# A split DMA transpose and chunked products for one batch, between two tiles of a fused attention and snake-MLP kernel

## The chip, the cores and the metric

The kernel runs on one core of one Trainium2 chip. The metric is the device time of one execution in microseconds, the median of several runs. The profile is of one execution and counts time from the start of its span, 294.8 us, which is a little shorter than the run's time.

Names used below: TensorE (PE in the profile, its weight loads PEld), VectorE (DVE), ScalarE (ACT), GpSimd (POOL), and SyncE (SP), which issues most of the DMAs. SBUF is the on-chip memory, PSUM the accumulator memory that TensorE writes.

## The reference

Linear attention over 8 batches of 8 heads, 576 tokens and 64 features a head, followed by an MLP on the 8 x 576 = 4608 tokens of 512 features:

```python
q_s = softmax(q, axis=-1)                 # over the 64 features
k_s = softmax(k, axis=2)                  # over the 576 tokens
kv  = einsum('bhsd,bhse->bhde', k_s, v)   # 64 x 64 for each head
a   = einsum('bhsd,bhde->bhse', q_s, kv)  # 576 x 64 for each head
x   = a.transpose(0, 2, 1, 3).reshape(4608, 512)
h   = x @ w_in                            # 512 -> 2048
g   = h + sin(alpha * h) ** 2 / alpha
out = g @ w_out                           # 2048 -> 512
```

(The reference also subtracts the maximum before each exponential and adds 1e-9 to the divisors.)

## The kernel before

The MLP works on nine tiles of 512 tokens. For each tile it makes 16 slots `h` of 128 x 512 (four matmuls each, the "first product", into PSUM tiles `hp`), a sine and a square, the combination `g`, and then four blocks of the output, 16 matmuls each (the "second product", PSUM tiles `op`). The attention of a batch has 576 tokens, 9 groups of 64; its result goes transposed into `xT`, from which the first product reads. Batch 2 fills columns 1152 to 1727 of `xT`, tile 2 reads columns 1024 to 1535.

The parts that the change touches:

```python
    def norm_q(b, engs):                       # softmax's division for q
        qe = A["qe", b]
        A["qn", b] = qn = att1.tile([128, J, 4 * D], BF16, name="qn")      # att1: one buffer
        qs = small.tile([128, J, 4], F32, name="qs")
        n = len(engs)
        w = 4 // n
        for h in range(n):
            cols = slice(h * w * D, (h + 1) * w * D)
            ...
            nc.vector.tensor_reduce(part, src, axis=AXL.X, op=ALU.add)
            nc.vector.reciprocal(part, part)
            engs[h].tensor_tensor(dst, src, part.unsqueeze(3).to_broadcast([128, J, w, D]), op=ALU.mult)

    TP = ((0, 6), (6, 9))

    def q_transpose(b, g, pool, eng):          # on TensorE, for batches 0 and 1
        ...
        for j in range(j0, j1):
            h, jj = divmod(j - j0, 3)
            for ii in range(2):
                nc.tensor.transpose(tp[:, h, 2 * jj + ii], qn[:, j, ii * 128:(ii + 1) * 128], identb)
        eng(qT[:, j0:j1].rearrange("p (h jj) ii c -> p h (jj ii) c", h=m), tp[:, 0:m, 0:6])

    def q_transpose_dma(b):                    # by DMA, for batches 2 to 7
        A["qT", b] = att2.tile([128, J, 2, 128], BF16, name="qT")
        nc.sync.dma_start(out=A["qT", b].rearrange("p j ii c -> p (j ii) c"),
                          in_=A["qn", b].rearrange("p j c -> p (j c)"), transpose=True)

    XO = ((0, 4), (4, 9))

    def attn_out(b, ii, half, pool, eng):      # q times kv: two matmuls and one evacuation
        qT, kt = A["qT", b], kbd[b % 2]
        j0, j1 = XO[half]
        n = (j1 - j0) * P                      # P = 64
        xp = pool.tile([128, 2, 512], F32, name="xp", tag="a")
        for e in range(2):
            nc.tensor.matmul(xp[:, e, 0:n], kt[:, e, ii], qT[:, j0:j1, ii, e * 64:(e + 1) * 64],
                             start=True, stop=True)
        c0 = (J * b + j0) * P
        eng(xT[:, 2 * ii:2 * ii + 2, c0:c0 + n], xp[:, :, 0:n])

    ...
    ps_h = ctx.enter_context(tc.tile_pool(name="ps_h", bufs=4, space=PSUM, reuse_waits="tile"))
    ps_o = ctx.enter_context(tc.tile_pool(name="ps_o", bufs=2, space=PSUM, reuse_waits="tile"))
    ps_a = ctx.enter_context(tc.tile_pool(name="ps_a", bufs=1, space=PSUM, reuse_waits="tile"))
    ...
    # between the first product of tile 1 and that of tile 2
    exp_q(2)
    exp_k(2)
    os = o_stream(1)                           # tile 1's 64 output matmuls, taken in parts
    take(os, 16)
    norm_q(2, [GP, V])
    exp_q(3)
    exp_k(3)
    load("v", v, 3)
    q_transpose_dma(2)
    cast_v(3, [GP, GP])
    nc.scalar.activation(zero, zero, AX.Sin)
    take(os, 16)
    kv_mm(2, 0, ps_a)
    kv_mm(2, 1, ps_a)
    kv_norm(2)
    norm_q(3, [GP])
    take(os, 26)
    for n in range(4):
        attn_out(2, n // 2, n % 2, ps_a, ACT_CP)
        take(os, (2, 2, 1, 1000)[n])
    q_transpose_dma(3)
    load_batch(4)
    ...
    for ni in range(nN):                       # tile 2's first product
        h_slot(2, ni, SQ2[ni], lag, lent)
        ...
```

Instructions of one engine run in the order of the program. The `evac_o` inside `o_stream` empties each output block with VectorE and issues two output DMAs.

Of the kernel before, what the change touches and what calls it, by code (L numbers as in the profile page):

```python
# [15 lines left out]
F32 = mybir.dt.float32  # L16
BF16 = mybir.dt.bfloat16
AX = mybir.ActivationFunctionType
ALU = mybir.AluOpType
AXL = mybir.AxisListType  # L20
# [3 lines left out]
def kernel(  # L24
# [14 lines left out]
    nc = tc.nc  # L39
    ctx.enter_context(nc.allow_non_contiguous_dma(reason="layout"))  # L40
    B, H, S, D = q.shape
# [3 lines left out]
    J = 9  # L45
    P = S // J
    nN = d_ff // 128
    MF = 512
# [7 lines left out]
    att1 = ctx.enter_context(tc.tile_pool(name="att1", bufs=1))  # L56
    att2 = ctx.enter_context(tc.tile_pool(name="att2", bufs=2))
# [8 lines left out]
    identb = singles.tile([128, 128], BF16, name="identb")  # L66
    xT = singles.tile([128, 4, NT], BF16, name="xT")
# [5 lines left out]
    kbd = [singles.tile([128, 2, 2, 128], BF16, name=f"kbd{n}") for n in range(2)]  # L73
    vb = [singles.tile([128, J, 4 * 65], BF16, name=f"vb{n}") for n in range(2)]

    def src_view(t, b):
        return t[b].rearrange("(i e) (p j) d -> (e p) i (j d)", e=2, j=J)
# [5 lines left out]
    staged = {}  # L83

    def load(name, t, b, halves=False, eng=nc.sync):
        st = stage.tile([128, 4, J, D], F32, name=f"st_{name}", tag="st")
        view = src_view(t, b)
        flat = st.rearrange("p i j d -> p i (j d)")
        if halves:
            for ii in range(2):  # L90
                eng.dma_start(out=flat[:, ii::2], in_=view[:, ii::2])
        else:
            eng.dma_start(out=flat, in_=view)
        staged[name, b] = st

    def load_batch(b):
        load("q", q, b)
        load("k", k, b)
        load("v", v, b)
# [6 lines left out]
    def load_wout(c):  # L106
        nc.gpsimd.dma_start(out=wout[:, 4 * c:4 * c + 4, :], in_=wout_v[:, 4 * c:4 * c + 4, :])


    A = {}  # L110
# [6 lines left out]
    def exp_q(b):  # L117
        A["qe", b] = att2.tile([128, J, 4 * D], BF16, name="qe")
        exp_to(A["qe", b], staged["q", b])
# [5 lines left out]
    def cast_v(b, engs):  # L125
        vv = vb[b % 2].rearrange("p j (i c) -> p i j c", i=4)
        for ii in range(2):
            engs[ii].tensor_copy(vv[:, 2 * ii:2 * ii + 2, :, 0:D], staged["v", b][:, ii::2])  # L128

    def norm_q(b, engs):  # L130

        qe = A["qe", b]
        A["qn", b] = qn = att1.tile([128, J, 4 * D], BF16, name="qn")
        qs = small.tile([128, J, 4], F32, name="qs")
        n = len(engs)
        w = 4 // n
        for h in range(n):
            cols = slice(h * w * D, (h + 1) * w * D)
            src = qe[:, :, cols].rearrange("p j (i d) -> p j i d", i=w)
            dst = qn[:, :, cols].rearrange("p j (i d) -> p j i d", i=w)  # L140
            part = qs[:, :, h * w:(h + 1) * w]
            nc.vector.tensor_reduce(part, src, axis=AXL.X, op=ALU.add)  # L142
            nc.vector.reciprocal(part, part)  # L143
            engs[h].tensor_tensor(dst, src, part.unsqueeze(3).to_broadcast([128, J, w, D]), op=ALU.mult)  # L144

    def kv_mm(b, ii, pool, split=False):

# [21 lines left out]

    TP = ((0, 6), (6, 9))  # L170

    def q_transpose(b, g, pool, eng):
        if g == 0:
            A["qT", b] = att2.tile([128, J, 2, 128], BF16, name="qT")
        qn, qT = A["qn", b], A["qT", b]
        j0, j1 = TP[g]
        m = (j1 - j0) // 3
        tp = pool.tile([128, 2, 8, 128], BF16, name="tp", tag="a")
        for j in range(j0, j1):
            h, jj = divmod(j - j0, 3)  # L180
            for ii in range(2):
                nc.tensor.transpose(tp[:, h, 2 * jj + ii], qn[:, j, ii * 128:(ii + 1) * 128], identb)
        eng(qT[:, j0:j1].rearrange("p (h jj) ii c -> p h (jj ii) c", h=m), tp[:, 0:m, 0:6])  # L183

    def q_transpose_dma(b):
        A["qT", b] = att2.tile([128, J, 2, 128], BF16, name="qT")
        nc.sync.dma_start(out=A["qT", b].rearrange("p j ii c -> p (j ii) c"),
                          in_=A["qn", b].rearrange("p j c -> p (j c)"), transpose=True)

    XO = ((0, 4), (4, 9))  # L190

    def attn_out(b, ii, half, pool, eng):
        qT, kt = A["qT", b], kbd[b % 2]
        j0, j1 = XO[half]
        n = (j1 - j0) * P
        xp = pool.tile([128, 2, 512], F32, name="xp", tag="a")
        for e in range(2):
            nc.tensor.matmul(xp[:, e, 0:n], kt[:, e, ii], qT[:, j0:j1, ii, e * 64:(e + 1) * 64],  # L198
                             start=True, stop=True)
        c0 = (J * b + j0) * P  # L200
        eng(xT[:, 2 * ii:2 * ii + 2, c0:c0 + n], xp[:, :, 0:n])  # L201


    G = {}
# [40 lines left out]
                                                         in_=o[64 * hf:64 * hf + 64, cols])  # L245


    ACT_CP, DVE_CP = nc.scalar.copy, nc.vector.tensor_copy
    V, GP = nc.vector, nc.gpsimd
    nc.scalar.dma_start(out=alpha_rows, in_=moe_alpha.rearrange("(no ni) -> no ni", ni=128))  # L250
    load("q", q, 0, halves=True)
# [3 lines left out]
    for ii, j0, j1 in VJ:  # L255
        nc.sync.dma_start(out=st[:, ii::2, j0:j1].rearrange("p i j d -> p i (j d)"),
                          in_=src_view(v, 0)[:, ii::2, j0 * D:j1 * D])
# [48 lines left out]
    ps_h = ctx.enter_context(tc.tile_pool(name="ps_h", bufs=4, space=PSUM, reuse_waits="tile"))  # L306

    def h_slot(t, ni, sq, lag, wide=None):
        hp = mm_h(t, ni, wide)
        lag.append((t, ni, hp, sine(t, ni, hp, sq)))  # L310

    def flush(lag, keep):
        while len(lag) > keep:
            combine(*lag.pop(0))
# [14 lines left out]
    def take(it, n=1000):  # L329
        for _ in range(n):  # L330
            if next(it, 0) == 0:
                return
# [4 lines left out]
    with tc.tile_pool(name="ps_e", bufs=2, space=PSUM, reuse_waits="tile") as ps_e:  # L337
        def lent():
            return ps_e.tile([128, 2, MF], F32, name="hh", tag="a")[:, 0]

        late = {3: ("q", q, 1, True), 6: ("k", k, 1, False), 8: ("v", v, 1, True)}
        for ni in range(nN):
            h_slot(0, ni, "PAPDPAPADPAPPDAP"[ni], lag, lent)
            flush(lag, 1)
            if ni in late:
                name, x, b, hv = late[ni]
                load(name, x, b, halves=hv, eng=GP)
            if ni == 11:
                load_wout(3)
        flush(lag, 0)  # L350

        exp_q(1)
        norm_q(1, [GP, V])
        exp_k(1)
        cast_v(1, [GP, GP])
        for name, x in (("q", q), ("k", k), ("v", v)):
            load(name, x, 2, eng=GP)
        accs = [ps_h.tile([128, dm], F32, name="hp", tag="h") for _ in range(4)]
        os = o_quad(0, accs, [DVE_CP, ACT_CP, DVE_CP, ACT_CP])
        take(os, 44)  # L360
        q_transpose(1, 0, ps_e, ACT_CP)
        nc.scalar.activation(zero, zero, AX.Sin)
        take(os, 2)
        q_transpose(1, 1, ps_e, DVE_CP)
        take(os, 2)
        kv_mm(1, 0, ps_e)
        kv_mm(1, 1, ps_e)
        kv_norm(1)
        take(os, 6)
        for ii in range(2):  # L370
            attn_out(1, ii, 0, ps_e, DVE_CP)
            attn_out(1, ii, 1, ps_e, ACT_CP)
            take(os, 3)
        take(os)
        load("q", q, 3)
        load("k", k, 3)

        for ni in range(nN):
            h_slot(1, ni, SQ[ni], lag, lent)
            flush(lag, 1)  # L380
        cast_v(2, [GP, GP])
        flush(lag, 0)

    ps_o = ctx.enter_context(tc.tile_pool(name="ps_o", bufs=2, space=PSUM, reuse_waits="tile"))
    ps_a = ctx.enter_context(tc.tile_pool(name="ps_a", bufs=1, space=PSUM, reuse_waits="tile"))
# [14 lines left out]
    os = o_stream(1)  # L400
# [2 lines left out]
    exp_q(3)  # L403
    exp_k(3)
    load("v", v, 3)
    q_transpose_dma(2)
    cast_v(3, [GP, GP])
    nc.scalar.activation(zero, zero, AX.Sin)
    take(os, 16)
    kv_mm(2, 0, ps_a)  # L410
    kv_mm(2, 1, ps_a)
    kv_norm(2)
    norm_q(3, [GP])
    take(os, 26)
    for n in range(4):
        attn_out(2, n // 2, n % 2, ps_a, ACT_CP)
        take(os, (2, 2, 1, 1000)[n])
    q_transpose_dma(3)
    load_batch(4)

# [18 lines left out]
    for t in range(3, nT):  # L439
        b = t + 1 if t + 1 < B else None  # L440
        os = o_stream(t - 1)
        done = 0
        for ni in range(nN):
            hp = mm_h(t, ni)
            if b is not None:
                if ni == 4:
                    q_transpose_dma(b)
                attn_back(b, ni - 5)
            s = sine(t, ni, hp, "A")
            combine(t, ni, hp, s)  # L450
            if b is not None and ni == 0:
                exp_q(b)
                exp_k(b)
                cast_v(b, [GP, GP])
                norm_q(b, [GP])
                if b + 1 < B:
                    load_batch(b + 1)
            want = 23 + 21 * ni // 8 if b is not None else 4 * (ni + 1)
            take(os, min(64, want) - done)
            done = min(64, want)  # L460
        take(os)

    take(o_stream(nT - 1), 48)
    for h in range(2):
        cols = slice(h * 256, h * 256 + 256)
# [34 lines left out]
```

The softmax here doesn't subtract the row's maximum and nothing guards it: scores larger than these inputs give would overflow.

## Time and profile before

| what | value |
|---|---|
| time, median of 3 runs | 296.62 us (296.46 to 296.97) |
| span of the profiled execution | 294.8 us |
| TensorE matmuls busy | 279.5 us, 95% |
| ScalarE busy | 228.1 us, 77% |
| VectorE busy | 185.9 us, 63% |
| GpSimd busy | 84.6 us, 29% |
| the six DMA transposes, issue to landing | 4.6 to 5.7 us, median 5.1 |
| the v load of batch 3 | issued at 69.30 us, used from 75.19 us |

In the lines quoted below, L187 is the DMA transpose (`qT<-qn`), L198 the products of q and kv (`xp`), L201 their evacuation into `xT`, L215 the first product (`hp`), L235 the second product (`op`), L142 to L144 the normalisation of q. An entry "x26" is a run of 26 instructions shown as one. Where square brackets end a line they give how long the engine stood idle before it and what it waited for. A busy TensorE is not TensorE at its peak, because matmuls are pipelined; the pitch from one to the next is shorter than the duration shown for one.

### The profile page before, as it was taken

The numbers are of one execution on the slowest core, as the hardware profiler recorded it, in microseconds if no ns is written. First come the engines' busy times: TensorE is split into PE (matmuls) and PEld (weight loads), VectorE is DVE, ScalarE is ACT, GpSimd is POOL, SyncE is SP. The second block draws the span as 40 slices with busy tenths as digits, with TensorE's granted clock in tenths as the row PEclk, the third lists the DMA queues.
The fourth block names the chain that finished last, engine by engine and source line by source line (L and its number), as shares of the span: only waits on it lengthen the run. The fifth ranks groups of instructions, "written<-read, shape, count | busy, mean of one in ns | idle before, by whom it ended". The sixth has DMA issues, their size and how long they took to land.

```text
span 294.8 us, 4250 instructions
## 1 busy us (share of the span) xinstructions
PE 279.5 (95%) x1576; PEld 132.4 (45%) x1576; DVE 185.9 (63%) x270; ACT 228.1 (77%) x320; POOL 84.6 (29%) x73
## 2 busy tenths in 40 slices
PE   2999999999799999999999999999999999999994
PEld 1544445444344444444444444444444444444443
DVE  3758955789638857865687568756875455555421
ACT  4679855999578899879987999799977777777500
POOL 0939590575665536000700061005000000000000
PEclk9999999999999999999999999999999999999999
DMA  7999989955859986108921794112411111111143
GB/s 261 281 191 207 366 234 364 390 189 165 183 85 323 392 282 139 28 21 290 330 50 36 235 337 98 36 39 60 91 38 36 36 36 38 36 36 37 46 99 72
DMA packets 35221, 45.77 MB, mean 155 GB/s; under 512 B 15856, under 2 KB 19712, under 8 KB 35200
## 3 DMA queue, kind: packets, MB, share of 16 engines
q1 hardware_dynamic: 29600, 34.09, 40.6%
q0 software_dynamic: 5408, 11.27, 14.9%
q8 instruction: 12, 0.20, 0.3%
q10 hardware_dynamic: 192, 0.14, 0.2%
q14 instruction: 9, 0.07, 0.1%
HBM read 36.71 MB, written 9.44 MB: 157 GB/s over the span
## 4 chain that ended last, share of the span: by engine, by line
PE 75%; DVE 9%; ACT 5%; POOL 3%; DMA 3%; issue 2%; ACTq 0%; SPq 0%
PE op L235 31%; PE hp L215 30%; PE hp L235 4%; DVE g L231 3%; PE xp L198 3%; PE warm L279 2%; POOL s L225 2%; DVE xT L201 2%; ACT s L221 2%; PE kvp L154 2%; DMA qT<-qn 2%; DMA st_q<-in_q_dram 1%; DVE o L241 1%; ACT xT L201 1%; PE op L468 1%
## 5 line engine op out<-in xcount | busy, mean ns | idle before, releaser
L231 DVE SCALAR_TENSOR_TENSOR g<-s,inva_sb,hp 128x512 bf16<-128x512 f32 x130 | 95.3, 746 | 65.1 <-ACT s L223 52.3
L215 PE MATMUL hp<-xT,win 128*128 128x512 bf16 x520 | 129.7, 379 | 0.3
L235 PE MATMUL op<-wout,g 128*128 128x512 bf16 x496 | 123.8, 379 | 0.0
L221 ACT ACTIVATE s<-hp,alpha_sb 128x512 f32<-128x512 f32 x130 | 87.8, 682 | 27.0 <-PE hp L215 23.0
L215 PEld LDWEIGHTS <-win 128*128 128x128 bf16 x576 | 56.1, 98 | 68.3 <-issue 2.3
L235 PEld LDWEIGHTS <-g 128*128 128x128 bf16 x560 | 54.0, 98 | 61.9 <-issue 1.0
L223 ACT ACTIVATE s<-s 128x512 f32<-128x512 f32 x112 | 70.5, 629 | 3.6
L144 POOL TENSOR_TENSOR qn<-qe,qs 128x2304 bf16<-128x2304 bf16 (+1 forms) x8 | 26.6, 3328 | 85.2 <-DVE qs L143 79.5
L225 POOL TENSOR_TENSOR s<-s 128x512 f32<-128x512 f32 x27 | 28.4, 1058 | 25.9 <-ACT s L221 25.7
L241 DVE COPY o<-op 128x512 f32<-128x512 f32 (+1 forms) x33 | 21.9, 663 | 14.2 <-PE op L235 11.8
L142 DVE TENSOR_REDUCE qs<-qe 128x18 f32<-128x1152 bf16 (+1 forms) x11 | 20.7, 1880 | 13.1 <-ACT qe L114 13.0
L114 ACT ACTIVATE qe<-st_q 128x1152 bf16<-128x1152 f32 x16 | 17.8, 1155 | 2.8 <-DMA st_q<-in_q_dram 2.7
L114 ACT ACTIVATE ke<-st_k 128x1152 bf16<-128x1152 f32 x16 | 17.7, 1150 | 2.5 <-DMA st_k<-in_k_dram 2.5
L128 POOL CAST vb<-st_v 128x1152 bf16<-128x1152 f32 x14 | 16.5, 1210 | 7.9 <-DMA st_v<-in_v_dram 7.9
L201 DVE CAST xT<-xp 128x512 bf16<-128x512 f32 (+1 forms) x22 | 16.5, 753 | 2.8 <-PE xp L198 2.7
L198 PE MATMUL xp<-qT,kbd 128*128 128x256 bf16 (+1 forms) x64 | 12.4, 285 | 4.2 <-ACT xT L201 1.8
L235 PE MATMUL hp<-wout,g 128*128 128x512 bf16 x64 | 15.1, 379 | 0.4 <-DVE g L231 0.3
L198 PEld LDWEIGHTS <-kbd 128*128 128x128 bf16 x64 | 6.0, 97 | 12.9 <-issue 5.7
L201 ACT CAST xT<-xp 128x512 bf16<-128x512 f32 (+1 forms) x10 | 6.3, 638 | 7.0 <-PE xp L198 6.9
L279 PE MATMUL warm<-qe,identb 128*128 128x512 bf16 x19 | 7.5, 562 | 2.8 <-ACT qe L114 2.8
L154 PE MATMUL kvp<-vb,ke 64*128 64x130 bf16 x288 | 9.8, 216 | 0.4 <-ACT qT L183 0.3
L114 ACT ACT_TABLE_LOAD x7 | 9.0, 1283 | 1.3 <-PEq L484 1.2
(51 smaller groups left out, 112.2 us busy)
## 6 DMA issues: line engine op xcount, KB each, us to landing
out_dram<-o SPq DMA_DIRECT2D x70, 128.0 KB, 2.4
st_q<-in_q_dram SPq DMA_DIRECT2D x5, 1152.0 KB, 6.3
st_k<-in_k_dram SPq DMA_DIRECT2D x5, 1152.0 KB, 8.7
st_v<-in_v_dram SPq DMA_DIRECT2D x5, 1152.0 KB, 10.7
st_k<-in_k_dram POOLq DMA_DIRECT2D x2, 1152.0 KB, 10.8
wout<-in_moe_w_out_dram POOLq DMA_DIRECT2D x4, 512.0 KB, 14.4
st_q<-in_q_dram SPq DMA_DIRECT2D x2, 576.0 KB, 4.6
st_k<-in_k_dram SPq DMA_DIRECT2D x2, 576.0 KB, 6.6
```

The costliest lines, as they stand in the source:

```text
L114: nc.scalar.activation(dst[:, :, ii * 128:(ii + 1) * 128].rearrange("p j (x d) -> p x j d", x=2), src[:, ii::2], AX.Exp)
L142: nc.vector.tensor_reduce(part, src, axis=AXL.X, op=ALU.add)
L144: engs[h].tensor_tensor(dst, src, part.unsqueeze(3).to_broadcast([128, J, w, D]), op=ALU.mult)
L198: nc.tensor.matmul(xp[:, e, 0:n], kt[:, e, ii], qT[:, j0:j1, ii, e * 64:(e + 1) * 64], start=True, stop=True)
L201: eng(xT[:, 2 * ii:2 * ii + 2, c0:c0 + n], xp[:, :, 0:n])
L215: nc.tensor.matmul(hp, win[:, ki, ni * 128:(ni + 1) * 128], xT[:, ki, t * MF:(t + 1) * MF], start=(ki == 0), stop=(ki == 3))
L221: nc.scalar.activation(s, hp, AX.Sin, scale=alpha_sb[:, ni:ni + 1])
L223: nc.scalar.activation(s, s, AX.Square)
L225: nc.gpsimd.tensor_tensor(s, s, s, op=ALU.mult)
L231: nc.vector.scalar_tensor_tensor(G[t][:, ni], in0=s, scalar=inva_sb[:, ni:ni + 1], in1=hp, op0=ALU.mult, op1=ALU.add)
L235: nc.tensor.matmul(acc, G[t][:, ni, j * 128:(j + 1) * 128], wout[:, ni, :], start=(ni == 0), stop=(ni == nN - 1))
L241: eng(o[:, cols], acc)
```

## The change

It rebuilds batch 2's attention between tile 1 and tile 2. The q of the batch is transposed by two DMAs instead of one, so that products on the first half of the heads need not wait for the second; for this, `qn` and `qT` are laid out with the half outermost, in all batches. The products of the first six token groups, which tile 2 reads, are made one 128-feature chunk at a time into the four PSUM banks of the first product, which are idle then, and evacuated by ScalarE and VectorE in turn. The products of the last three groups, which only tile 3 reads, follow together in the attention's own PSUM buffer, evacuated by VectorE at once. Fewer output matmuls are taken ahead of the products and more between and after them.

The new layout makes two instructions out of one in two other places: the evacuation of the TensorE transposes (batches 0 and 1), and GpSimd's normalisation of q where it does a whole batch (from batch 3 on).

```diff
     def norm_q(b, engs):
-        qe = A["qe", b]
-        A["qn", b] = qn = att1.tile([128, J, 4 * D], BF16, name="qn")
+        qe = A["qe", b].rearrange("p j (ii x d) -> p ii j x d", ii=2, x=2)
+        A["qn", b] = qn = att1.tile([128, 2, J, 2 * D], BF16, name="qn")
         qs = small.tile([128, J, 4], F32, name="qs")
...
+        if len(engs) == 1:
+            nc.vector.tensor_reduce(qs, A["qe", b].rearrange("p j (i d) -> p j i d", i=4), axis=AXL.X, op=ALU.add)
+            nc.vector.reciprocal(qs, qs)
+        for ii in range(2):
+            part = qs[:, :, 2 * ii:2 * ii + 2]
+            if len(engs) == 2:
+                nc.vector.tensor_reduce(part, qe[:, ii], axis=AXL.X, op=ALU.add)
+                nc.vector.reciprocal(part, part)
+            engs[ii % len(engs)].tensor_tensor(qn[:, ii].rearrange("p j (x d) -> p j x d", x=2), qe[:, ii],
+                                               part.unsqueeze(3).to_broadcast([128, J, 2, D]), op=ALU.mult)
...
     def q_transpose(b, g, pool, eng):
...
-        eng(qT[:, j0:j1].rearrange("p (h jj) ii c -> p h (jj ii) c", h=m), tp[:, 0:m, 0:6])
+                nc.tensor.transpose(tp[:, h, ii, jj], qn[:, ii, j], identb)
+        for ii in range(2):
+            eng(qT[:, ii, j0:j1].rearrange("p (h jj) c -> p h jj c", h=m), tp[:, 0:m, ii, 0:3])
...
+    def q_transpose_dma(b, halves=False):
+        for ii in range(2) if halves else (slice(0, 2),):
+            out, in_ = q_tile(b)[:, ii], A["qn", b][:, ii]
...
+            nc.sync.dma_start(out=out, in_=in_, transpose=True)
...
+    def attn_chunk(b, c, j0, j1, xp):
+        ii, e = divmod(c, 2)
+        nc.tensor.matmul(xp, kbd[b % 2][:, e, ii], A["qT", b][:, ii, j0:j1, e * 64:(e + 1) * 64],
+                         start=True, stop=True)
...
-    q_transpose_dma(2)
+    q_transpose_dma(2, halves=True)
...
     norm_q(3, [GP])
-    take(os, 26)
-    for n in range(4):
-        attn_out(2, n // 2, n % 2, ps_a, ACT_CP)
-        take(os, (2, 2, 1, 1000)[n])
+    take(os, 20)
+
+    c0 = J * 2 * P
+    for c in range(4):
+        xp = ps_h.tile([128, MF], F32, name="hp", tag="h")[:, 0:6 * P]
+        attn_chunk(2, c, 0, 6, xp)
+        (ACT_CP, DVE_CP)[c % 2](xT[:, c, c0:c0 + 6 * P], xp)
+        take(os, 1)
+    xp = ps_a.tile([128, 2, 512], F32, name="xp", tag="a")[:, :, 0:6 * P]
+    for c in range(4):
+        attn_chunk(2, c, 6, 9, xp[:, c // 2, (c % 2) * 3 * P:(c % 2 + 1) * 3 * P])
+    DVE_CP(xT[:, :, c0 + 6 * P:c0 + 9 * P].rearrange("p (h c) n -> p h c n", h=2),
+           xp.rearrange("p h (c n) -> p h c n", c=2))
+    take(os)
     q_transpose_dma(3)
```

More of the change, by code (lines that the diff above doesn't have):

```diff
@@ L127, in cast_v @@
         for ii in range(2):
-            engs[ii].tensor_copy(vv[:, 2 * ii:2 * ii + 2, :, 0:D], staged["v", b][:, ii::2])
+            engs[ii](vv[:, 2 * ii:2 * ii + 2, :, 0:D], staged["v", b][:, ii::2])
     def norm_q(b, engs):
-        qe = A["qe", b]
-        A["qn", b] = qn = att1.tile([128, J, 4 * D], BF16, name="qn")
+        qe = A["qe", b].rearrange("p j (ii x d) -> p ii j x d", ii=2, x=2)
+        A["qn", b] = qn = att1.tile([128, 2, J, 2 * D], BF16, name="qn")
         qs = small.tile([128, J, 4], F32, name="qs")
[L135 to L144, printed above, removed]
+        if len(engs) == 1:
[8 more added lines that the diff above has]
+                                               part.unsqueeze(3).to_broadcast([128, J, 2, D]), op=ALU.mult)
     def kv_mm(b, ii, pool, split=False):
@@ L170, with q_tile @@
     TP = ((0, 6), (6, 9))
+    def q_tile(b):
+        if ("qT", b) not in A:
+            A["qT", b] = att2.tile([128, 2, J, 128], BF16, name="qT")
+        return A["qT", b]
     def q_transpose(b, g, pool, eng):
-        if g == 0:
-            A["qT", b] = att2.tile([128, J, 2, 128], BF16, name="qT")
-        qn, qT = A["qn", b], A["qT", b]
+        qn, qT = A["qn", b], q_tile(b)
         j0, j1 = TP[g]
         m = (j1 - j0) // 3
-        tp = pool.tile([128, 2, 8, 128], BF16, name="tp", tag="a")
+        tp = pool.tile([128, 2, 2, 4, 128], BF16, name="tp", tag="a")
         for j in range(j0, j1):
@@ L181, in q_transpose, with q_transpose_ii @@
             for ii in range(2):
-                nc.tensor.transpose(tp[:, h, 2 * jj + ii], qn[:, j, ii * 128:(ii + 1) * 128], identb)
-        eng(qT[:, j0:j1].rearrange("p (h jj) ii c -> p h (jj ii) c", h=m), tp[:, 0:m, 0:6])
[L185 to L188, printed above, removed]
+                nc.tensor.transpose(tp[:, h, ii, jj], qn[:, ii, j], identb)
+        for ii in range(2):
+            eng(qT[:, ii, j0:j1].rearrange("p (h jj) c -> p h jj c", h=m), tp[:, 0:m, ii, 0:3])
+    def q_transpose_ii(b, ii, j0, j1, tp):
+        for j in range(j0, j1):
+            nc.tensor.transpose(tp[:, j - j0], A["qn", b][:, ii, j], identb)
+    def q_transpose_dma(b, halves=False):
+        for ii in range(2) if halves else (slice(0, 2),):
+            out, in_ = q_tile(b)[:, ii], A["qn", b][:, ii]
+            if not halves:
+                out, in_ = out.rearrange("p ii j c -> p (ii j) c"), in_.rearrange("p ii j c -> p ii (j c)")
+                in_ = in_.rearrange("p ii c -> p (ii c)")
+            else:
+                in_ = in_.rearrange("p j c -> p (j c)")
+            nc.sync.dma_start(out=out, in_=in_, transpose=True)
     XO = ((0, 4), (4, 9))
@@ L197, in attn_out @@
         for e in range(2):
-            nc.tensor.matmul(xp[:, e, 0:n], kt[:, e, ii], qT[:, j0:j1, ii, e * 64:(e + 1) * 64],
+            nc.tensor.matmul(xp[:, e, 0:n], kt[:, e, ii], qT[:, ii, j0:j1, e * 64:(e + 1) * 64],
                              start=True, stop=True)
@@ L245, in evac_o @@
                                                          in_=o[64 * hf:64 * hf + 64, cols])
-    ACT_CP, DVE_CP = nc.scalar.copy, nc.vector.tensor_copy
+    ACT_CP, DVE_CP, GP_CP = nc.scalar.copy, nc.vector.tensor_copy, nc.gpsimd.tensor_copy
     V, GP = nc.vector, nc.gpsimd
@@ L354 @@
         exp_k(1)
-        cast_v(1, [GP, GP])
+        cast_v(1, [GP_CP, GP_CP])
         for name, x in (("q", q), ("k", k), ("v", v)):
@@ L380 @@
             flush(lag, 1)
-        cast_v(2, [GP, GP])
+        cast_v(2, [GP_CP, GP_CP])
         flush(lag, 0)
@@ L405 @@
     load("v", v, 3)
-    q_transpose_dma(2)
-    cast_v(3, [GP, GP])
+    q_transpose_dma(2, halves=True)
+    cast_v(3, [GP_CP, GP_CP])
     nc.scalar.activation(zero, zero, AX.Sin)
@@ L453 @@
                 exp_k(b)
-                cast_v(b, [GP, GP])
+                cast_v(b, [GP_CP, GP_CP])
                 norm_q(b, [GP])
```

## The prediction

> **What bounds the kernel now.** I read the page's shares of busy time first, then the chain of waits, then the stage around batch 2 (63 to 84 us) in order of time, and last the DMA share in half-microsecond windows.
>
> ```profile
> PE 279.5 (95%) x1576; PEld 132.4 (45%) x1576; DVE 185.9 (63%) x270; ACT 228.1 (77%) x320; POOL 84.6 (29%) x73
> ```
>
> TensorE is the bound: it is busy for 279.5 of 294.8 us, and from 101 us on the chain is almost nothing but its matmuls. So the change can win only where TensorE stands still. One such place is batch 2; the chain around it, with start, length and what it is:
>
> ```profile
> 71.10 1.98 DVE qn L144
> ...
> 73.13 5.36 DMA qT<-qn
> 78.49 0.14 issue
> 78.62 0.39 PE xp L198 x2
> ...
> 79.04 0.59 ACT xT L201
> ...
> 82.41 0.70 ACT xT L201
> ...
> 83.15 1.47 PE hp L215 x6
> ```
>
> The reader is to see that for ten microseconds the chain leaves the dense matmuls: normalised q, its transpose by DMA, then matmul and evacuation in turn. The same stretch in order of time, with the idle time and its releaser in brackets:
>
> ```profile
> 69.72 2.13 POOL L144 TENSOR_TENSOR qn<-qe,qs 128x1152 bf16<-128x1152 bf16 x1 [1.48 <-DVE qs L143]
> 71.78 5.79 PE L235 MATMUL op<-wout,g 128*128 128x512 bf16 x26
> 78.62 0.38 PE L198 MATMUL xp<-qT,kbd 128*128 128x256 bf16 x2 [1.06 <-DMA qT<-qn]
> 79.67 0.43 PE L198 MATMUL xp<-qT,kbd 128*128 128x320 bf16 x2 [0.24 <-ACT xT L201]
> 80.89 0.38 PE L198 MATMUL xp<-qT,kbd 128*128 128x256 bf16 x2 [0.35 <-ACT xT L201]
> 81.94 0.43 PE L198 MATMUL xp<-qT,kbd 128*128 128x320 bf16 x2 [0.46 <-ACT xT L201]
> ```
>
> 26 matmuls in 5.79 us, the last shown with 0.379, give a pitch of (5.79 - 0.379)/25 = 0.216 us. TensorE has two troubles. The 58th output matmul ends at about 77.5 and the transpose lands at 78.49: 1.06 idle. Then one buffer serves four products (`ps_a` has one), so each waits for ScalarE to empty it: 0.24 + 0.35 + 0.46 = 1.05. A third wait carries no bracket: the first slot of tile 2 starts its first two matmuls at 82.42, and its third comes only at 83.15, after the last evacuation. Counted back by two pitches, the tile effectively starts at 83.15 - 0.43 = **82.72**. This is the number to move.
>
> The DMA during the wait (the last two columns are the share of the 16 engines and GB/s):
>
> ```profile
> 73.50:74.00 0.50, 0.50 (x4) 0.25 (x3) 0.47 (x3) 0.50 (x2) 0.00 (x0) 1.00 0.99 392
> 74.00:74.50 0.50, 0.50 (x4) 0.24 (x3) 0.49 (x2) 0.50 (x1) 0.00 (x0) 1.00 0.67 224
> 75.00:75.50 0.50, 0.50 (x4) 0.24 (x3) 0.50 (x1) 0.50 (x1) 0.31 (x1) 1.00 1.17 216
> 78.00:78.50 0.50, 0.00 (x0) 0.00 (x0) 0.39 (x1) 0.00 (x0) 0.00 (x0) 1.00 0.97 234
> ```
>
> Until about 74.2 the load of v of batch 3, issued at 69.30, runs at 392 GB/s; after a short dip the transpose holds the engines full until it lands.
>
> **What the Trainium skill says.** "Perfetto Trace Analysis", Optimizing Tensor Performance, wants independent matmul groups to rotate through different PSUM banks so that evacuation overlaps the next matmuls: the three waits on ScalarE are that rule broken. The same page, DMA Optimizations, says that splitting a DMA lets some of it start sooner if the engines are generally idle; here they are not, at a share near 1 from 71.5 to 78.5. "DMA: Bandwidth & Descriptors", Queues, rings and completion order, says that SP owns one ring on each DMA engine and that descriptors there are consumed in order. The trace agrees so far as the transpose's rate appears only when the load's is gone. So I let a transpose that is issued earlier stand behind that load.
>
> **The change, part by part.**
>
> *Halves of the transpose.* The first half of qn is done by GpSimd at 69.72 + 2.13 = 71.85, the second by VectorE at 73.08. So the first issue moves from 73.13 to about 71.9. What does that buy? A transpose of batch 4, at 113.02, had no other traffic beside it: its share of the engines rises at about 114.25 and falls at about 118.25, so 1.2 us from issue to first data and 4.0 us of data for the whole, 2.0 for a half. The first half could start at 73.1, but the v load holds the ring until about 74.2: it runs 74.2 to 76.2, and lands at about 76.4. The second follows without a gap, 76.2 to 78.2, and lands at about 78.35. So the last byte gains only the dip, 0.15 us; the gain is that half of the data is there two microseconds earlier.
>
> *TensorE's order.* The count of output matmuls ahead of the first product falls from 26 to 20: they end at 71.78 + 20 x 0.216 = 76.1. Chunks 0 and 1 need only the first half: a wait of about 0.4 to 76.5, then chunk (384 columns, 384/512 x 0.216 = 0.16), one output matmul (0.22), chunk, output matmul: 0.76, to 77.3. Chunk 2 needs the second half: landing at 78.35 plus the 0.13 from landing to matmul that the chain shows gives 78.48, so 1.2 idle. After that chunk, output matmul, chunk, output matmul are 0.76; four remainders of 192 columns 4 x 0.08 = 0.32; the last 8 output matmuls 1.73. Tile 2 starts at 78.48 + 2.81 = **81.29**, against 82.72: 1.43 sooner. The columns streamed are the same in both, 4 x 384 + 4 x 192 = 4 x 576 = 2304.
>
> *Evacuation.* Each chunk has its own bank of `ps_h`, empty since tile 1 ended, so TensorE waits for none. ScalarE takes 0.586 for 512 elements and 0.692 for 640, 0.83 ns an element, so about 0.48 for 384; VectorE, at 0.69 and 0.82, about 0.55. VectorE is busy until 78.4 (sums of batch 3, then an output copy at 77.70), then chunk 1, and chunk 3 at about 79.1 to 79.7, the remainder of 768 elements 0.95 more, to 80.6. Tile 2 needs columns 1024 to 1535, and the chunks of 384 end exactly there, 1152 + 384 = 1536: they are ready at 79.7, well before 81.29, and the remainder is not needed until tile 3. Both waits on evacuation vanish.
>
> *Losses elsewhere.* The transposes of batches 0 and 1 on TensorE now have two evacuations each. ScalarE: 1.439 for 1536 elements is 0.164 of fixed cost by the 0.83 above; one fixed cost more, less the overlap of about 0.08 that two neighbouring exps show (1.15 each, 2.22 for two), is 0.08. VectorE's 0.558 copy grows by about as much. The chain runs over VectorE's copy in batch 0 (13.25) and ScalarE's in batch 1 (42.55): 2 x 0.08 = 0.16 lost. GpSimd's normalisation is 2 x 2.13 instead of 4.05 from batch 3 on, 0.2 later; the later transposes land 2 us before their product (about 118.3 for 120.63), so it is hidden.
>
> *Downstream.* GpSimd may overwrite qn only when both halves have landed: 78.5 + 4.26 = 82.8. Tile 2's first square comes at 81.29 + 0.86 + 0.7 = 82.85, so it just misses the collision. The transpose of batch 3 and the loads behind it move forward with the last output, and the rest of the kernel is TensorE in order. I pass the whole 1.43 on. Sum: 1.43 - 0.16 = 1.27, and 296.62 - 1.27 = **295.3 us**.
>
> **The rivals.** *The halves are quick*: they slip in beside the v load and the second lands at 77.1. For it: the issue is 1.2 us earlier, and the share in the v load's time is at places only 0.8 to 0.9. Against it: bytes conserve, and the share is 1 from 71.5 on. TensorE would then lose 0.4 only: tile 2 at about 80.1, a gain of 2.6, 294.1 us. *The DMA wait takes the ladder's place*: two descriptor streams cost more than one, the second half lands at 79.3 or later, and idle time at chunk 2 eats the gain: about 296.2. For it: 1.2 us from issue to first data are paid twice if the two do not overlap. Against it: the second is issued long before the first ends. *The gain is swallowed later*: tile 2's stage has its own waits on ScalarE and VectorE (0.55 before a product at 95.23, for lack of buffers); if GpSimd's squares, held by the longer normalisation, set its pace, half is lost: 296.0.
>
> **Range and chances.** The first rival has about 15 in 100, the two others together 30, and the base the rest; hence 294.1 to 296.4. 2% is 5.9 us, more than all TensorE idle time in this stage (2.5), so "faster by over 2%" and "slower by over 2%" have about one chance in a hundred each.
>
> **What would show it.** Two transposes in the DMA queue, the first landing near 76.4 and the second near 78.35; chunk 0 waiting about 0.4, chunk 2 about 1.2 on the DMA, no product of batch 2 on ScalarE; tile 2's first slot without a break, near 81.4 (with 0.1 from batches 0 and 1 in it). The dense chain from 101 us on should sit about 1.3 earlier. I am wrong if the second half lands before 77.5 or after 79, or if tile 2 starts 1.4 earlier and its end does not.

## The result and the profile after

The changed kernel takes 293.87 us (293.15 to 294.47) against 296.76 us of the kernel before: a ratio of 0.990, 95% interval 0.987 to 0.993. That is 2.9 us less; 1.3 was predicted, with 294.1 as the low end of the range. A repetition, reported below with the experiments, gave 0.989 (0.987 to 0.990).

The chain of waits of the changed kernel around batch 2 (start, length, what):

```profile
71.68 4.42 PE op L255 x20
76.10 0.32 PE hp L220
...
77.04 0.32 PE hp L220
...
78.29 1.73 PE op L255 x8
80.01 1.74 PE hp L235 x8
```

The DMA, the normalisation and ScalarE's evacuations are gone from it; it is TensorE's own work until tile 2 runs, with two short waits hidden in the entries for `op`. The same in order of time, with the idle time in brackets where there is any:

```profile
71.71 3.26 SPq L202 DMA_TRANSPOSE qT<-qn  x2
76.10 0.32 PE L220 MATMUL hp<-qT,kbd 128*128 128x384 bf16 x1
76.46 0.48 ACT L440 CAST xT<-hp 128x384 bf16<-128x384 f32 x1 [0.34 <-PE hp L220]
77.04 0.32 PE L220 MATMUL hp<-qT,kbd 128*128 128x384 bf16 x1
77.72 4.21 POOL L143 TENSOR_TENSOR qn<-qe,qs 128x1152 bf16<-128x1152 bf16 x2 [0.35 <-POOL vb L128]
78.14 1.01 DVE L440 CAST xT<-hp 128x384 bf16<-128x384 f32 x2
79.06 0.95 DVE L445 CAST xT<-xp 128x768 bf16<-128x768 f32 x1
79.85 3.62 PE L235 MATMUL hp<-xT,win 128*128 128x512 bf16 x16
```

The 20 output matmuls end at 71.61 + 20 x 0.216 = 75.93, chunk 0 runs at 76.10, chunk 2 at 77.04, where its two predecessors and their output matmuls end at 76.10 + 0.76 = 76.86: 0.17 and 0.18 us lost, each just after a landing. Tile 2 starts at 79.85 and its first 16 matmuls run without a break. Last, the two transposes of batch 2 by themselves (duration of issue least, median, longest; then issue to landing):

```profile
L202 SPq DMA_TRANSPOSE qT<-qn x2: 1392/1580/1767, 71.7 to 73.2; - x2
DMA to landing us min/median/max: 3.8/4.1/4.3
```

The first, issued at 71.7, lands 4.3 later at 76.0 (chunk 0 follows at 76.10); the second, issued at 73.2, lands 3.8 later at 77.0 (chunk 2 at 77.04).

Since every run reaches the middle of the kernel at a slightly different moment, the stages are compared by TensorE's marks in each trace: first output matmul of tile 1, of tile 2, and the last matmul of all.

| kernel | tile 1's outputs to tile 2's outputs, us | tile 2's outputs to last matmul | last matmul to end of span |
|---|---|---|---|
| before (two traces) | 37.07, 37.05 | 189.9 | 4.22, 4.70 |
| changed (two traces) | 34.38, 34.68 | 189.9 | 3.69, 3.66 |

So 2.4 to 2.7 us come from the stage that the change rebuilds, nothing from the long dense part behind it, and 0.5 to 1.0 from the end of the kernel, where nobody looked for it.

### The profile page after: what moved, and what is told of

Read it like the earlier page. It is cut to its first block, busy times and chain, and to the rows that moved or that the text cites. A ratio compares the mean times of both kernels' runs of the same rounds, so it can differ in the third digit from the quotient of the medians.

```text
span 291.4 us, 4261 instructions
## 1 busy us (share of the span) xinstructions
PE 278.9 (96%) x1576; PEld 132.4 (45%) x1576; DVE 188.0 (65%) x275; ACT 226.7 (78%) x320; POOL 84.9 (29%) x78
## 4 chain that ended last, share of the span: by engine, by line
PE 80%; DVE 8%; ACT 5%; POOL 3%; issue 2%; DMA 1%; ACTq 0%
PE op L255 35%; PE hp L235 31%; PE hp L255 4%; DVE g L251 3%; PE warm L299 2%; PE kvp L154 2%; POOL s L245 2%; DVE xT L215 2%; ACT s L241 2%; PE xp L212 2%; DMA st_q<-in_q_dram 1%; PE op L498 1%; PE hh L235 1%; ACT s L243 1%; DVE o L261 1%
## 5 line engine op out<-in xcount | busy, mean ns | idle before, releaser
L143 POOL TENSOR_TENSOR qn<-qe,qs 128x1152 bf16<-128x1152 bf16 x13 | 27.4, 2127 | 83.7 <-DVE qs L137 67.6
L114 ACT ACTIVATE qe<-st_q 128x1152 bf16<-128x1152 f32 x16 | 17.9, 1156 | 2.9 <-DMA st_q<-in_q_dram 2.9
L136 DVE TENSOR_REDUCE qs<-qe 128x36 f32<-128x2304 bf16 x5 | 12.8, 2553 | 10.8 <-ACT qe L114 10.7
L212 PE MATMUL xp<-qT,kbd 128*128 128x256 bf16 (+1 forms) x56 | 10.8, 285 | 2.1 <-DVE xT L215 1.0
L154 PEld LDWEIGHTS <-ke 64*128 64x128 bf16 x288 | 8.2, 93 | 3.8 <-issue 2.1
L212 PEld LDWEIGHTS <-kbd 128*128 128x128 bf16 x56 | 5.3, 97 | 9.2 <-issue 3.8
```

The lines of the kernel that those rows point to most:

```text
L114: nc.scalar.activation(dst[:, :, ii * 128:(ii + 1) * 128].rearrange("p j (x d) -> p x j d", x=2), src[:, ii::2], AX.Exp)
L143: engs[ii % len(engs)].tensor_tensor(qn[:, ii].rearrange("p j (x d) -> p j x d", x=2), qe[:, ii], part.unsqueeze(3).to_broadcast([128, J, ...
L154: nc.tensor.matmul(kvp[:, e, ii * 130:(ii + 1) * 130], ke[r, j, ii * 128:(ii + 1) * 128], vt[r, j, ii * 130:(ii + 1) * 130], start=(j == 0 ...
L212: nc.tensor.matmul(xp[:, e, 0:n], kt[:, e, ii], qT[:, ii, j0:j1, e * 64:(e + 1) * 64], start=True, stop=True)
```

## The experiments

The theories after the result. **Issue**: a DMA transpose lands about 2 us after SyncE has finished issuing it; in halves, only half of the issue stands behind the last part of qn. **Transfer** (the prediction's own): the data of both halves pass the DMA engines one after the other behind the v load, 2.0 us each. **Overlap**: two transposes in flight move faster than one. **Layout**: the new arrangement of qn and qT makes the transposes faster. Beside these, how much is the split and how much the banks.

### One transpose, the rest as changed

```diff
-    q_transpose_dma(2, halves=True)
+    q_transpose_dma(2)
```

> The changed kernel with batch 2's transpose left whole (one DMA), everything else as changed. If the split is what brings the time: the whole is issued at about 72.9 and lands at about 78.2, TensorE waits some 2.3 us at the first chunk, tile 2 starts at about 81.9 instead of 79.85, and the time is about 296.0. If the separate banks bring it and the split little: tile 2 starts before 80.5 and the time stays under 294.7.

Measured 0.998 of before (0.996 to 0.999), 296.12 us. In order of time, the first chunk:

```profile
79.58 0.32 PE L220 MATMUL hp<-qT,kbd 128*128 128x384 bf16 x1 [2.23 <-DMA qT<-qn]
79.74 0.38 PE L255 MATMUL op<-wout,g 128*128 128x512 bf16 x1
79.96 0.32 PE L220 MATMUL hp<-qT,kbd 128*128 128x384 bf16 x1
```

TensorE waits 2.23 us for the DMA, as expected, and after that for nothing until tile 2. The stage takes 36.44, only 0.6 less than before: without the split the banks remove the ladder of waits but the DMA takes its place. The median hides a part of the gain, since six of the 20 runs (296.9 to 297.9 us) were granted a mean clock of only 0.992 to 0.994, the others (295.2 to 296.5) 0.997 or more.

### The halves, with the old products

```diff
-    take(os, 20)
-    ... four chunks into ps_h, ScalarE and VectorE in turn; the remainder into ps_a
+    take(os, 26)
+    for n in range(4):
+        attn_out(2, n // 2, n % 2, ps_a, ACT_CP)
+        take(os, (2, 2, 1, 1000)[n])
```

> The changed kernel with the old products of batch 2 (26 output matmuls first, four products through one PSUM buffer, all evacuated by ScalarE), the transpose still in two halves. If split and banks each bring a part: no wait on the DMA any more, but the three waits on ScalarE (0.24 to 0.46 each) and the break in tile 2's first slot return; the products begin at about 77.2, tile 2 starts effectively at about 81.3, and the time is about 295.3. If the split alone brings it: under 294.5.

Measured 0.994 (0.992 to 0.996), 294.89 us. The products in order of time:

```profile
78.07 0.38 PE L212 MATMUL xp<-qT,kbd 128*128 128x256 bf16 x2
79.12 0.43 PE L212 MATMUL xp<-qT,kbd 128*128 128x320 bf16 x2 [0.24 <-ACT xT L215]
80.33 0.38 PE L212 MATMUL xp<-qT,kbd 128*128 128x256 bf16 x2 [0.35 <-ACT xT L215]
81.39 0.43 PE L212 MATMUL xp<-qT,kbd 128*128 128x320 bf16 x2 [0.46 <-ACT xT L215]
```

The wait on the DMA is gone and the ladder stands to the hundredth as before. The stage takes 35.87, 1.2 less. The two parts alone give 0.6 and 1.2, together 2.4 to 2.7: each removes one of two waits, and the first alone brings up the other.

### The layout alone

```diff
-    q_transpose_dma(2, halves=True)
+    q_transpose_dma(2)
     ... and the old products, as in the experiment before
```

> Only the new layout of qn and qT (with its doubled evacuations in batches 0 and 1 and GpSimd's two-part normalisation), neither split nor chunks. By the prediction's loss term 296.76 + 0.16 = 296.9. If the layout itself makes the transposes faster (the rival that explains the early landing by it): the whole transpose of batch 2 lands over 0.5 us sooner after its issue than the 5.4 of before, and the time is below 296.4.

Measured 0.998 (0.997 to 0.999), 296.13 us, 0.7 under before where the prediction had 0.16 over. But the transpose lands 5.3 after its issue (5.4 before), and the stage takes 37.04 (37.07 before). The layout theory falls: the layout does nothing for the transposes. What it gains lies outside the stage, and is taken up below.

### Halves for the later batches too

```diff
-    q_transpose_dma(3)
+    q_transpose_dma(3, halves=True)
...
-                    q_transpose_dma(b)
+                    q_transpose_dma(b, halves=True)
```

> The changed kernel with the transposes of batches 3 to 7 in halves too. Batch 4's (near 110 us) has no load beside it and landed whole 4.6 us after its issue. If the descriptor issue on SyncE sets the pace (a half costs about 1.4 us of issue and lands about 2 us after that): the first half lands 3.3 to 3.6 us after the first issue, the second 4.6 to 5.0 after it, no sooner than the whole. If two transposes in flight move faster than one (overlap): the second lands under 4.1 us after the first issue. The time should be that of the changed kernel within 0.4 us under both, as these transposes are hidden.

Measured 0.992 (0.990 to 0.994), 294.53 us. In the loop (batches 4 to 7) the two halves turned out not to be in flight together: GpSimd finishes them 2.1 us apart, so the run says nothing about overlap. It gives something better, a half by itself. Batch 7's transpose near 200 us, in this kernel and then in the kernel before:

```profile
L202 SPq DMA_TRANSPOSE qT<-qn x2: 1279/1288/1298, 200.5 to 202.6; - x2
...
DMA to landing us min/median/max: 3.3/3.3/3.3
```

```profile
L187 SPq DMA_TRANSPOSE qT<-qn x1: 2761/2761/2761, 204.3 to 204.3; - x1
...
DMA to landing us min/median/max: 4.6/4.6/4.6
```

From the end of the issue to the landing it is 3.3 - 1.3 = 2.0 for a half and 4.6 - 2.8 = 1.8 for the whole. Halving the transpose saves 1.3 us of landing, close to the 1.5 of issue that it saves, and leaves the rest as it is. The data are halved too, so this run alone does not tell the issue from a faster transfer; the next one does.

### The halves in the other order

```diff
-        for ii in range(2) if halves else (slice(0, 2),):
+        for ii in (1, 0) if halves else (slice(0, 2),):
...
-    for c in range(4):
+    for c in (2, 3, 0, 1):
         xp = ps_h.tile(...)
```

> The changed kernel with the halves in the other order: VectorE's half of qn, which is ready last (72.9 in the changed kernel's trace), is transposed first, GpSimd's behind it, and the chunks run in the order 2, 3, 0, 1. If the issue sets the pace: it begins 1.2 us later than in the changed kernel, ends 1.4 + 1.5 us on, and the second landing is 5.0 to 5.3 us after the first issue, about 0.9 us later against the end of the v load than the 2.0 us of the changed kernel; tile 2 starts about 0.9 later. If the end of the v load sets the pace (descriptors wait in the ring and then drain at the engines' speed): both halves still land about 1 and 2 us after the v load, and tile 2 starts within 0.3 of where it did.

Measured 0.991 (0.990 to 0.993), 294.87 us. Issue, v load and chunks in order of time:

```profile
73.06 2.80 SPq L202 DMA_TRANSPOSE qT<-qn  x2
...
75.00 2.26 POOL L128 CAST vb<-st_v 128x1152 bf16<-128x1152 f32 x2 [3.22 <-DMA st_v<-in_v_dram]
76.55 0.32 PE L220 MATMUL hp<-qT,kbd 128*128 128x384 bf16 x1 [0.35 <-DMA qT<-qn]
...
78.14 0.32 PE L220 MATMUL hp<-qT,kbd 128*128 128x384 bf16 x1 [0.67 <-DMA qT<-qn]
```

The v load ends at 75.0 as ever, but the landings move out with the issue: 1.5 and 3.1 us after that end, where the changed kernel had 1.0 and 2.0. From first issue to second landing it is 78.1 - 73.1 = 5.0. The stage takes 35.38, 0.7 to 1.0 longer than the changed kernel's. The issue sets the pace of the last landing; the end of the v load does not.

A transfer of the right size behind the v load falls with it. A whole transpose is 128 x 2304 x 2 bytes, 590 KB; at the 216 GB/s of the single transpose this is 2.7 us, 1.4 for a half, and with it the prediction's own sum would have given 74.2 + 2.7 + 0.15 = 77.1 for the second landing (an estimate). But then both orders should land alike, and the reversed one is 0.7 to 1.1 later. The engines show it too, from 75.0 to 76.0 (last two columns: DMA share and GB/s):

```profile
75.00:75.50 0.50, 0.50 (x4) 0.25 (x3) 0.50 (x1) 0.50 (x1) 0.50 (x1) 1.00 1.14 203
75.50:76.00 0.50, 0.50 (x4) 0.20 (x2) 0.50 (x1) 0.50 (x1) 0.50 (x1) 1.00 1.08 202
```

The changed kernel moves 281 and 259 GB/s in the same windows (shown below). There the first half's issue had ended at 73.1, before the v load was through; here the halves are still being issued until 75.9.

### The v load behind the transposes, in halves and whole

```diff
-    load("v", v, 3)
     q_transpose_dma(2, halves=True)      # second run: q_transpose_dma(2)
+    load("v", v, 3)
```

> The changed kernel with the v load of batch 3 issued behind the two transposes, so that no load is in front of them. If the issue sets the pace: the first half lands 3.2 to 3.4 us after its issue (4.3 with the load in front), the second 4.6 to 4.8 after the first issue (5.3 with the load). If the transfer does (4.0 us of data for the whole, as the prediction had it): the second lands over 5.0 after the first issue even here. The v load comes later and GpSimd's cast and normalisation with it, so the time may rise by 1 to 2 us; the landings are what is asked.

> As the one before, but the transpose whole. Without the load in front it should land 4.6 us after its issue, as batch 4's does, against 5.3 with it: that would put 0.7 us of the wait on the load. If the load costs it nothing, 5.3 again.

One execution each: 298.97 and 301.17 us. In halves, the first lands 3.5 after its issue at 72.7, the second 3.2 after its issue at 74.2: 4.7 after the first issue and 1.9 after the end of its own. That is what the issue theory said, and under the transfer theory's 5.0. It also answers the overlap theory, which wanted under 4.1: two transposes in flight with nothing in front of them end no sooner than a whole one. Whole, the transpose lands 4.7 after its issue, against 5.3 with the load in front: the load costs a whole transpose 0.6.

The times are a warning. In halves, the late v holds GpSimd's cast until 82.17 and its squares until 88.56, and TensorE stands idle for 3.4 us:

```profile
90.43 5.26 PE L235 MATMUL hp<-xT,win 128*128 128x512 bf16 x16 [3.42 <-DVE g L251]
```

The 16 matmuls behind the idle time take 5.26 us, where the kernel before has 3.63 for 16 of the same kind: TensorE's granted clock is 0.50 from about 90.5 to 93.5, and with the whole transpose, after 3.38 us of idle time, from 90.5 to 97. So tile 2's own stage grows from 17.9 to 23.1 and 24.3 us by the wait and by the lower clock behind it. Why the clock fell is not tested.

### 23 output matmuls ahead, and the changed kernel beside it

```diff
-    take(os, 20)
+    take(os, 23)
```

> The changed kernel with 23 output matmuls ahead of the first chunk instead of 20. In the changed kernel's trace TensorE loses about 0.17 us at chunk 0 and 0.2 at chunk 2; with 3 x 0.216 = 0.65 more work ahead both halves have landed before their chunks, so tile 2 starts 0.3 to 0.4 sooner after the start of tile 1's outputs, and the time is 0.3 below the changed kernel's if nothing else moves. If those small gaps are not waits on the DMA: no change.

> The changed kernel, unchanged, on the same chip as the next one: 0.990 of the kernel before, as measured.

> 23 output matmuls ahead of the first chunk, beside the changed kernel on one chip. By the traces tile 2's outputs start 0.31 us sooner after tile 1's (34.07 against 34.38), so 0.1% less than the changed kernel. If the much lower ratio that it showed on another chip is a property of the kernel: 0.5% less.

The first run gave 0.985 (0.983 to 0.986). On one chip with the changed kernel: 0.987 (0.985 to 0.989), 293.31 us, against 0.989 (0.987 to 0.990), 293.58 us. The intervals overlap, so the times don't part the two. The traces do: the stage takes 34.07 and 34.04, against 34.38 and 34.68. The larger value of the changed kernel is a trace in which the second half landed later and chunk 2 waited:

```profile
77.47 0.32 PE L220 MATMUL hp<-qT,kbd 128*128 128x384 bf16 x1 [0.34 <-DMA qT<-qn]
```

So 20 is slightly too few: with 23 the stage is 0.3 to 0.6 us shorter, in two traces of each.

### The end of the kernel

A second trace of the kernel before and of the layout alone, then the two by-products of the layout, each alone in the kernel before:

```diff
     # normalisation, old layout: GpSimd alone does two halves
-            engs[h].tensor_tensor(dst, src, ...)          # once for 2304 elements
+            engs[h % len(engs)].tensor_tensor(dst, src, ...)   # twice for 1152
```

```diff
     # evacuation of the TensorE transposes, old layout
-        eng(qT[:, j0:j1]..., tp[:, 0:m, 0:6])
+        ... the same elements in two instructions
```

> The kernel before, unchanged, for a second trace of it. From the last matmul to the end of the span it took 4.22 us in the first trace and 3.68 to 3.84 in the nine traces of kernels with the new layout. If that is a property of the kernel before: 4.1 or more again. If it is chance: under 3.9.

> The layout alone, unchanged, for a second trace, beside the one of the kernel before on the same chip. The layout alone measured 0.2% less time than before, where the prediction had 0.16 us more; in its first trace nothing between the start of tile 1's outputs and tile 2's is shorter. If the gain is in the end of the kernel: 0.4 us shorter from the last matmul to the end of the span again. If it is in the first 64 us: tile 1's outputs start earlier than in the kernel before's new trace.

> The kernel before, with only GpSimd's normalisation of q in two instructions from batch 3 on (old layout). Both traces of the kernel before take 4.22 and 4.70 us from the last matmul to the end of the span, every kernel with the new layout 3.64 to 3.84. If this part is what shortens the end: 3.6 to 3.9 here. If not: 4.2 or more. By the prediction's terms the time itself should not change (296.8).

> The kernel before, with only the evacuations of the TensorE transposes of batches 0 and 1 in two instructions (old layout). If this part is what shortens the end: 3.6 to 3.9 us from the last matmul to the end of the span here, otherwise 4.2 or more. By the prediction's loss term the time rises by 0.16 (296.9); the changed kernel's trace shows 0.06 to 0.07 in each batch.

From the last matmul to the end of the span: kernel before 4.70 (4.22 in the first trace), layout alone 3.69 (3.77 in the first), split normalisation 4.17, split evacuation 3.71. All twelve traces with the new layout, which has the split evacuation in it, show 3.64 to 3.84. The waits of SyncE's queue in the last 5 us show which wait it is; the kernel before in its two traces, then the split evacuation:

```profile
SPq L495 <- DMA out_dram<-o: 1.8, 1, 1.8
```

```profile
SPq L495 <- DMA out_dram<-o: 2.3, 1, 2.3
```

```profile
SPq L499 <- DMA out_dram<-o: 1.2, 1, 1.2
```

The wait for the last output DMA is 0.6 to 1.1 us shorter, though nothing in the program about that DMA differs. It came with the two-instruction evacuation, which works at 13 and 44 us. The times agree weakly: 0.998 (0.997 to 0.999) for the split evacuation, 1.001 (1.000 to 1.002) for the split normalisation. The first 64 us are not the place: tile 1's outputs start at 63.72 in the kernel before's new trace and at 63.67 in the layout's. The cause stays open: one trace of each of the two parts shows with which part the shorter end comes, not why.

## Why the prediction was wrong

**The bound and the place: right.** TensorE set the time, its idle time around batch 2 was what the change could win, and what was won there arrived whole at the last matmul (189.9 us from tile 2's outputs in both kernels).

**The first half: nearly right.** Issue 71.7 and landing 76.0, where 71.9 and 76.4 were predicted; the wait at chunk 0 was 0.17, not 0.4. That the load holds the ring fits: a half with nothing in front landed 3.2 to 3.5 after its issue, this one 4.3.

**The second half: wrong, and this is the step that failed.** "The second follows without a gap, 76.2 to 78.2, and lands at about 78.35": it landed at 77.0. The term was 2.0 us of data for a half behind the first; the two halves landed 1.0 apart. It came from the share of the DMA engines in batch 4, which rises at 114.25 and falls at 118.25, and that was misread. The transpose itself lands 4.6 after its issue at 113.02, so at 117.6; the share that goes on until 118.25 belongs to two output DMAs issued at 115.84. I had the landing of 4.6 in the same profile and did not hold the two against each other. This corrects the half only to (117.6 - 114.25)/2 = 1.7. The larger part of the error is that a share just over 1 was taken for a full engine. The changed kernel's windows (the last two columns again are share and GB/s):

```profile
75.00:75.50 0.50, 0.50 (x4) 0.20 (x2) 0.50 (x1) 0.50 (x1) 0.40 (x1) 1.00 1.27 281
75.50:76.00 0.50, 0.50 (x3) 0.20 (x2) 0.50 (x1) 0.49 (x2) 0.50 (x1) 1.00 1.28 259
76.00:76.50 0.50, 0.50 (x4) 0.21 (x3) 0.50 (x1) 0.16 (x2) 0.50 (x2) 1.00 1.51 322
```

The same 16 engines now move 259 to 322 GB/s, where the single transpose had 216 and the reversed halves 202 to 203. (Some of these packets can be an output DMA's, issued at 75.06, but from 74.75 to 75.00 the rate was already 282.) So "bytes conserve, and the share is 1" proved nothing: 216 GB/s was not all that the engines could move of a transpose.

What the runs put in its place is the issue. With nothing in front, a landing comes 1.8 to 2.1 us after the end of its issue, in halves and whole, and it comes later when the issue is later, in the reversed order (2.2 after the end of the last issue). Behind the v load it is more: 2.3 to 2.6 for the whole in the two traces of the kernel before, 2.9 for the first half and 2.0 to 2.3 for the second in the two of the changed kernel. The whole transpose begins its issue when VectorE has finished its part of qn, about 73.1, and the second half when the first half's issue is over, at 73.2; the whole then needs 2.8 to 3.0 us of issue, the half 1.8 here and 1.3 to 1.4 without the load. Counted from tile 1's outputs, the last issue ends 0.8 to 1.0 us sooner than before and the last landing is 1.0 to 1.3 sooner, so the issue carries most of it. The rest is what the load no longer costs the last landing; no run tests that by itself.

The Trainium skill has the notion, which I passed over: "Perfetto Trace Analysis", What "DMA-bound" means, names the issuing sequencer as a bound of its own, whose profiled window is the generation of descriptors. The prediction also bent the same page's DMA Optimizations: the page ties idle engines to the whole being complete sooner, not to a part starting sooner. Here the DMA share was near 1, and both came sooner.

In the sum: predicted landing 78.35, measured 77.0, 1.35 less (0.17 of it because this trace reaches tile 1's outputs that much sooner); the wait at chunk 2 was 0.18 instead of 1.2. Tile 2 thus started at 79.85 instead of 81.29.

**The rivals.** "The halves are quick" named the landing (77.1), tile 2's start (80.1) and the time (294.1) almost exactly, and got 15 in 100. It was right for another reason, and in the time partly by luck, since it knew nothing of the shorter end. Its reason was slipping in beside the v load; but from 73 to 74 the engines move 401 to 410 GB/s in the changed kernel and 392 to 424 before, the load's own rate. The earlier issue, which it also named, is what counted. My reason against it was the share.

**Evacuation: right.** 0.48 on ScalarE, 1.01 for VectorE's two, 0.95 for the remainder, no wait on any of them.

**Losses: right in the traces.** ScalarE's pair takes 1.50 instead of 1.44 and VectorE's 0.62 instead of 0.56, so 0.06 each where 0.08 was predicted. They were more than paid back by the shorter end, which no step of the prediction could have foreseen.

**Downstream: right in the cost, and nearly in the collision.** GpSimd's normalisation ends at 77.72 + 4.21 = 81.93, and the first square, ready at about 81.6, starts then, 0.3 late, where the prediction had it just miss. It cost nothing: from tile 2's first matmul to its outputs it is 17.93 in the changed kernel. The 18.22 of the kernel before contain the break in the first slot that is now gone.

**The whole**: 1.43 predicted for the stage, 2.4 to 2.7 measured; 0.5 to 1.0 more at the end of the kernel. The stage alone would have brought the time to 294.1 to 294.4 (an estimate, 296.76 less the stage's gain); the unforeseen end carried it below the range.

## What to carry to other kernels

Take a transfer's cost from its own landing times, and split each into issue and the rest, before reading anything out of the DMA share: a window of busy DMA engines can hold somebody else's packets, and a share near 1 does not say that no more would fit. Splitting a DMA whose issue is long paid here because one part of its source was ready early, so that only the last part's issue was left behind the last producer. Two waits in a row, here the DMA and the ladder of evacuations, are worth more removed together: alone they gave 0.6 and 1.2 us, together 2.4 to 2.7.

## What was not expected of the hardware

A DMA transpose of 128 x 2304 bf16 with nothing beside it took 2.8 us to issue and landed 1.8 to 1.9 us after that; one of 128 x 1152 took 1.3 and landed 2.0 after. A load of 1.15 MB in front cost the whole transpose another 0.6 us. Two halves behind such a load, with the first fully issued before the load was through, moved at up to 282 GB/s before any output was issued, where transposes just being issued moved at 202 to 216. After 3.4 us without matmuls TensorE's granted clock was 0.50 for 3 us in one trace and 6.5 us in another. The wait for the last output DMA differed by 0.6 to 1.1 us between the kernel before (two traces) and one that differs from it only in two evacuations within the first 46 us (one trace); the cause is open.
